# The hidden layer's last pair in the wide form, first pairs in another order, and gates moved to ScalarE

## The chip, the cores and the metric

The kernel runs on one core of one Trainium2 chip. A core has TensorE (PE in the profile; its weight loads are PEld), VectorE (DVE), ScalarE (ACT), GpSimd (POOL) and SyncE (SP). Each of them takes its instructions in the order in which the program wrote them. The metric is the device time of one execution in microseconds (us), lower being better. Before the change it is 849.36 us, the median of three runs (848.73 to 850.72).

## The reference

Two stages in float32. The first is attention with a mask from hashes: queries and keys of 4 batches, 8 heads, 768 positions and 64 features are hashed to 6 bits each, and a query sees the keys of its own bucket only. The second is a feed-forward layer on the 3072 x 512 result:

```python
def _moe_ref(x, w_in, w_out) -> np.ndarray:
    h = x @ w_in              # 3072 x 512 by 512 x 2048
    r = np.maximum(h, 0.0)
    g = r * r
    return (g @ w_out).astype(np.float32)
```

The change touches the second stage only, and the squares of a guard that looks for large inputs.

## The kernel before

Attention fills the first 314 us. Then the 3072 tokens are worked in three chunks of 1024 (`i` = 0, 1, 2, called chunk 0, 1, 2 here). Each chunk has a hidden part (x @ w_in and the gate, which is max(h, 0) * h) and a projection (`project`, g @ w_out).

**Products with seven multiplications.** Both use a form of Strassen's algorithm, in which a 2 x 2 block product takes 7 block products, some of sums of blocks. `product` writes one such step: seven groups of matmuls in the order 11, 21, t2, t1, t3, 22, t4, with sums of the moving operand called t1 to t4. Several of them go on accumulating in the same PSUM bank, so a bank's value is copied out by ScalarE between two groups (`keep`, the tiles `one`, `two`, `three`, `five`), and the later group must wait for that copy. With two levels, 49 products take the place of 64.

**The hidden part.** Chunk 0 uses one level (`hidden`). In chunks 1 and 2 the 16 row blocks of the hidden layer are made in four pairs of units (n = 0 to 3), each pair in two halves (`half` = 0, 1). A half has a weight unit `w_unit`. The results go to four tiles b11, b12, b21, b22, each with 8 slices; pair n makes slices r0 = n and r = 4 + n. `outer_steps` gives the first-level ("outer") groups, of two 128x512 matmuls each, in a bank `acc0`. `inner_steps` gives a second-level product of seven 128x256 matmuls, cut into four steps 0 to 3. A to E are five such inner products. `hidden_wide` (pairs 0 to 2) has 4 outer groups and 5 inner products; `hidden_pair` (pair 3) has 8 outer groups and the 3 inner products A, B, C.

An inner product's steps use two banks: one accumulates over steps 0 to 3 with a copy by ScalarE after each, the other is used in step 0 and again in steps 1 and 2. There are eight banks: `side_bank` 0 and 1 and two each of acc0, acc1, acc2. The step's copies land in tiles `h` (5 buffers), `three` (2), and `five` (1 buffer, for D).

**What follows a pair.** VectorE adds the inner result to the outer one and applies the gate in one instruction (`put`, `gated`). `gate_in` is the gate on ScalarE: a Relu and a Square in place. Differences b_t = b12 - b11 and b12 = b22 - b12, and `inner_sums` for the projection, follow on VectorE. What is left over from a pair is kept as a list of steps and written between the next pair's steps by `behind(m)`. D and E, the inner products with own factors, need the sums of a weight unit (`sum_unit`; made in chunk 1 on VectorE, stored by GpSimd to `w_in_49`, loaded in chunk 2), and sums of x (`sums_inner`).

**The projection.** Seven products (k = 0 to 6) take b11, b12, b_t, b22, b21, then b11 and b_t again, which by then hold a second and a fourth sum. Weights come as `leaf` tiles (7 buffers): five are loaded ahead, from the last half but one of the hidden part, by SyncE in chunk 0 and by ScalarE's queue in chunks 1 and 2; the others always by ScalarE's queue. `hook` is what VectorE does after the second group of a product.

**The guard.** `mark` squares a piece of q and k on ScalarE with an accumulated sum (32 in all, two buffers; each then has GpSimd load a later piece). Their maximum is read in chunk 2's product 4.

The order of everything is written out by hand: the order of calls in these functions is the order in each engine's queue.

Of the kernel before, what the change touches and what calls it, by code (L numbers as in the profile page):

```python
# [34 lines left out]
def kernel(  # L35
# [686 lines left out]
    def load_unit(n, pool=p_i):  # L722

        if n < NCHUNK * NR and n not in w_unit:
# [3 lines left out]
            if n < NR or pair == NQ - 1:  # L728
                m = 7 if n < NR else 4
                nc.sync.dma_start(out=w[:, 0:m], in_=w_in_7[r, :, 0:m])  # L730
                return
# [6 lines left out]
            if n >= 2 * NR:  # L738
                nc.sync.dma_start(out=five_six(w), in_=w_in_49[pair, :, 3 + half])
# [4 lines left out]
    def sum_unit(n):  # L744


        if NR <= n < 2 * NR and n % NR < NR - 2:
# [6 lines left out]
            nc.gpsimd.dma_start(out=w_in_49[pair, :, 3 + half], in_=five_six(w))  # L754
# [15 lines left out]
    with tc.manual_schedule():  # L770
# [201 lines left out]
        def product(n, w, at, bt, c11, c12, c21, c22, hook=None, last=False, beside=None, cuts=1):  # L972
# [16 lines left out]
            def keep(of, name):  # L989
                t = p_r.tile([P, 512], FP32, name=name, bufs=KEPT[name])[:, 0:w]  # L990
                nc.scalar.copy(out=t, in_=acc[of])  # L991
                return t
# [121 lines left out]
        w_inner, t_inner, spots, snaps, now, behind_pair = {}, {}, {}, {}, {}, {}  # L1114
# [77 lines left out]
        def sums_inner(i, js):  # L1192

            for j in js:
                y11, y12, y21, y22 = quarters_x(i, j)
                if j < 3:
                    tile = p_y.tile([P, NQ, QN], FP32, name=f"t{j}", **({"bufs": 2} if j < 2 else {}))
                    t = [tile[:, m] for m in range(NQ - 1)] + [y12]
                    spots[i, j] = tile[:, NQ - 1]
                else:  # L1200
# [3 lines left out]
                t_inner[i, j] = t  # L1204
# [5 lines left out]
        def inner_steps(i, j, side, w):  # L1210

            t1, t2, t4, t3 = t_inner[i, j]
            y11, _, y21, y22 = quarters_x(i, j)
            if i not in snaps:
                snaps[i] = [side_bank(m)[:, 0:QN] for m in range(2)]
            one = three = spots[i, side]
            hs = {}

            def new(unit):
                name = "five" if (j, unit) == (3, 0) else "three" if j == 4 else None
                if name:
                    return p_r.tile([P, 512], FP32, name=name, bufs=KEPT[name])
                return new_h()

            def mul(out, a, b, start, stop):
                nc.tensor.matmul(  # L1228
                    out=out, lhsT=w(a), rhs=b, start=start, stop=stop, skip_group_check=True
                )  # L1230

            def step_0():
                a0, a1 = (
                    ps_m.tile([P, 512], FP32, name=f"acc{m}")[:, 0:QN] for m in (0 if j == 4 else 1, 2)
                )
                mul(a0, 0, y11, True, False)
                nc.scalar.copy(out=one, in_=a0)
                mul(a1, 1, y21, True, True)
                hs[0] = new(0)
                nc.vector.tensor_tensor(out=hs[0][:, 0:QN], in0=a1, in1=one, op=ALU.add)  # L1240
                hs["a0"] = a0

            def step_1():
                last = hs["last"] = (
                    ps_m.tile([P, 512], FP32, name="acc2")[:, 0:QN] if j == 4 else snaps[i][side]
                )
                mul(hs["a0"], 4, t2, False, False)
                nc.scalar.copy(out=hs[0][:, QN:HN], in_=hs["a0"])
                mul(last, 3, t1, True, False)
                hs[1] = new(1)  # L1250
                nc.scalar.copy(out=hs[1][:, QN:HN], in_=last)

            def step_2():
                mul(hs["a0"], 5, t3, False, False)
                nc.scalar.copy(out=three, in_=hs["a0"])
                mul(hs["last"], 6, y22, False, True)

            def adds():
                for unit, by in (0, hs["last"]), (1, three):
                    add_in(hs[unit][:, QN:HN], by)  # L1260

            def step_3():
                mul(hs["a0"], 2, t4, False, True)
                nc.scalar.copy(out=hs[1][:, 0:QN], in_=hs["a0"])

            def put(unit, out, other):
                add_in(hs[unit], other)
                gated(out, hs[unit])

            return step_0, step_1, step_2, step_3, put, adds, hs  # L1270
# [43 lines left out]
        def hidden_wide(i, n, half):  # L1314

            r0, r = n, NQ + n
            w, acc, add, keep = outer_steps(i, n, half)
            own = own_factors(w, half)
            if half == 0:
                load_inner(i, n + 1)  # L1320
                load_third_inner(i, n + 1, nc.sync)
                now["A"] = inner_steps(i, 0, 0, w_inner[i, n][0])
                if n == 0:
                    sums_inner(i, (3,))
                now["D"] = inner_steps(i, 3, 1, lambda a: own[a])
            A, D = now["A"], now["D"]
            u0 = D[6]
            add(acc, 0, "11", True, False)
            one = keep(acc, "one")
            if half == 0:  # L1330
                A[0]()
                D[0]()
                if n == 0:
                    mark()
                    sums_inner(i, (4,))
                behind(0)
            else:
                B, C = inner_steps(i, 2, 0, w_inner[i, n][2]), inner_steps(i, 1, 1, w_inner[i, n][1])
                E = inner_steps(i, 4, 2, lambda a: own[a])
                B[0]()  # L1340
                C[0]()
                E[0]()
                A[4](1, b11[:, r], one)
                behind(2)
# [641 lines left out]
```

## Time and profile before

| what | value |
|---|---|
| median of the runs | 849.36 us |
| the profiled execution | 851.49 us |
| its span in the profile | 849.9 us |
| granted TensorE clock | 0.999 |
| TensorE busy | 841.6 us (99%) |
| VectorE busy | 758.5 us (89%) |
| ScalarE busy | 439.8 us (52%) |
| chunk 1, four pairs of the hidden part | 495.14 to 584.93 us |
| chunk 2, four pairs of the hidden part | 669.82 to 758.62 us |
| last chunk's projection starts | 758.62 us |

The profile is one execution, of 851.49 us; its span, 849.9 us, counts from the first to the last recorded instruction. Busy times of matmuls are modelled, so a short wait of TensorE hides in them and shows better as the distance between two pieces of the chain. In the rows, `L1228` is a line of the kernel, `out<-in` are tile names, and a bracket gives the idle time of the engine before that row and what ended it. A matmul in float32 counts as two instructions.

### The profile page before, as it was taken

Reading aid. Unit: us, or ns where it says so; the run is one execution under the profiler, and the core shown is the slowest. Engines: PE = TensorE matmul, PEld = TensorE weight load, DVE = VectorE, ACT = ScalarE, POOL = GpSimd, SP = SyncE. Lnnn points to the kernel's source line nnn. Section 1 sums busy time; section 2 is a strip of 40 time slices with the busy share of each in tenths; the row PEclk is TensorE's granted clock in tenths of the full one; section 3 lists DMA queues with packets and bytes.
Section 4 is the critical chain, followed back from the end, with each engine's and each line's share of the span. In section 5 each row is a group of like instructions: output and inputs, shape, how many; then the busy total and the mean of one; then the engine's idle time right before and its main releaser. Section 6 shows DMA issues by size and latency. Waiting matters only on the chain.

```text
span 849.9 us, 17478 instructions
## 1 busy us (share of the span) xinstructions
PE 841.6 (99%) x6698; PEld 555.4 (65%) x6698; DVE 758.5 (89%) x1087; ACT 439.8 (52%) x833; POOL 171.0 (20%) x289
## 2 busy tenths in 40 slices
PE   9999999999999999999999999999999999999997
PEld 4444444444475445544788877767888777768885
DVE  4898999999999988989899989988988988888876
ACT  5887777878777762222211146775232457753210
POOL 1321121303221201643121220001211300021103
PEclk9999999999999999999999999999999999999999
DMA  9966999989996426999977994418878964157666
GB/s 185 201 130 138 185 186 201 207 173 224 249 245 202 158 69 245 330 312 306 359 254 220 275 226 145 146 50 292 298 214 244 247 207 145 51 169 213 201 166 128
DMA packets 237304, 174.10 MB, mean 205 GB/s; under 512 B 165224, under 2 KB 195248, under 8 KB 237216
## 3 DMA queue, kind: packets, MB, share of 16 engines
q1 hardware_dynamic: 196976, 90.14, 43.3%
q0 software_dynamic: 16992, 44.02, 16.5%
q10 hardware_dynamic: 23248, 38.78, 14.7%
q8 instruction: 54, 0.88, 0.5%
q14 instruction: 34, 0.28, 0.1%
HBM read 129.51 MB, written 42.73 MB: 203 GB/s over the span
## 4 chain that ended last, share of the span: by engine, by line
PE 95%; DMA 2%; DVE 1%; ACTq 0%; issue 0%; ACT 0%; POOL 0%; SPq 0%; POOLq 0%; DVEq 0%
PE acc L984 40%; PE st L478 18%; PE xo L532 14%; PE acc L1228 10%; PE acc L1298 8%; PE last L1228 3%; PE tot L589 1%; PE hash L396 1%; DMA bits<-signed 1%; DMA out_dram<-h 1%; PE tp L342 0%; DMA qk_nat<-in_q_dram 0%; ACTq L1499 0%; DVE h L1522 0%; DVE o L1288 0%
## 5 line engine op out<-in xcount | busy, mean ns | idle before, releaser
L484 ACT ACTIVATE e<-st 128x768 f32<-128x768 f32 x192 | 155.5, 810 | 56.8 <-PE st L478 52.5
L532 PE MATMUL xo<-e,v_nat 64*64 64x385 f32 (+1 forms) x1520 | 156.7, 483 | 0.0
L984 PE MATMUL acc<-b,leaf 128*128 128x256 f32 x600 | 133.1, 379 | 0.0
L984 PEld LDWEIGHTS acc<-b,leaf 128*128 128x128 f32 x600 | 113.9, 190 | 16.1 <-issue 0.5
L478 PE MATMUL st<-feat 64*64 64x384 f32 x1056 | 109.3, 483 | 0.0
L444 POOL DMA_DIRECT2D bits<-signed x120 | 62.1, 522 | 196.5 <-ACT signed L433 194.7
L532 PEld LDWEIGHTS xo<-e,v_nat 64*64 64x64 f32 (+1 forms) x1520 | 58.5, 133 | 65.7 <-issue 54.7
L984 PE MATMUL acc<-t,leaf 128*128 128x256 f32 x336 | 76.1, 379 | 0.0
L984 PEld LDWEIGHTS acc<-t,leaf 128*128 128x128 f32 x336 | 63.7, 190 | 9.1 <-issue 0.3
L478 PE MATMUL st<-bits 64*64 64x384 bf16 x768 | 65.9, 324 | 0.4 <-DMA bits<-signed 0.4
L520 DVE TENSOR_TENSOR total<-total,e 128x1536 f32<-128x1536 f32 x32 | 56.0, 1750 | 7.6 <-ACT e L484 6.9
L1028 POOL DMA_DIRECT2D raw_qk<-in_q_dram x32 | 17.3, 541 | 212.3 <-ACT raw_qk L1033 209.8
L520 DVE TENSOR_TENSOR t_x<-t_x,e 128x1536 f32<-128x1536 f32 x32 | 55.8, 1744 | 3.9 <-ACT e L484 3.8
L478 PEld LDWEIGHTS st<-feat 64*64 64x64 f32 x1056 | 39.8, 133 | 25.6 <-issue 21.7
L984 PE MATMUL acc<-x,w_unit 128*128 128x512 f32 (+1 forms) x144 | 56.5, 546 | 0.0
L984 PE MATMUL acc<-b_t,leaf 128*128 128x256 f32 x240 | 53.8, 379 | 0.0
L991 ACT COPY two<-acc 128x256 f32<-128x256 f32 (+1 forms) x29 | 12.5, 431 | 75.2 <-PE acc L984 59.7
L1076 DVE SCALAR_TENSOR_TENSOR b<-h 128x512 f32<-128x512 f32 x72 | 49.1, 691 | 2.2
L991 ACT COPY one<-acc 128x256 f32<-128x256 f32 (+1 forms) x29 | 12.5, 431 | 72.6 <-PE acc L984 53.3
L984 PEld LDWEIGHTS acc<-b_t,leaf 128*128 128x128 f32 x240 | 45.6, 190 | 6.2
L478 PE MATMUL st<-t_x 64*64 64x384 f32 x480 | 48.9, 482 | 0.0
L478 PEld LDWEIGHTS <-bits 64*64 64x64 bf16 x768 | 24.6, 107 | 35.2 <-issue 32.8
(234 smaller groups left out, 1537.8 us busy)
## 6 DMA issues: line engine op xcount, KB each, us to landing
leaf<-w_out ACTq DMA_DIRECT2D x142, 256.0 KB, 3.4
raw<-in_moe_w_in_dram SPq DMA_DIRECT2D x8, 1024.0 KB, 6.4
raw<-in_moe_w_out_dram SPq DMA_DIRECT2D x8, 1024.0 KB, 7.5
w_unit<-w_in SPq DMA_DIRECT2D x8, 896.0 KB, 8.5
w_out<-sums POOLq DMA_DIRECT2D x16, 448.0 KB, 7.4
v_nat<-in_v_dram SPq DMA_DIRECT2D x16, 384.0 KB, 5.1
x_all<-x_raw SPq DMA_DIRECT2D x16, 384.0 KB, 3.2
raw_qk<-in_q_dram POOLq DMA_DIRECT2D x32, 192.0 KB, 3.6
```

Source lines behind the costliest of these rows:

```text
L396: nc.tensor.matmul(out=banks[g * NR_B:(g + 1) * NR_B, h, 0:HS], lhsT=projs[rows, h * D:h * D + NR_B], rhs=feat[pr][rows, w, c * HS:(c + 1) ...
L444: nc.gpsimd.dma_start(out=t[h * D:h * D + NBITS + 1, w, c * HS:(c + 1) * HS], in_=signed[pr % 2][at:at + NBITS + 1, h],)
L478: nc.tensor.matmul(out=st[k * HK:(k + 1) * HK, h, 0:HS], lhsT=src[1][rows, key], rhs=src[0][rows, cut], start=first, stop=not first, skip_ ...
L484: nc.scalar.activation(out=key_of(pr, kt)[:, :, i, 0:HS], in_=st[:, :, 0:HS], func=ACTF.Exp, scale=scale)
L520: nc.vector.tensor_tensor(out=totals[pr], in0=totals[pr], in1=e, op=ALU.add)
L532: return nc.tensor.matmul(out=outs[pr][h * D:(h + 1) * D, c, 0:HS + 1], lhsT=nat[pr, "v_nat"][rows, h, kt * D:(kt + 1) * D], rhs=key_of(pr ...
L984: nc.tensor.matmul(out=acc[to][:, at_c], lhsT=a(i), rhs=b(i)[:, at_c], start=first and i == 0, stop=last and i == n - 1, skip_group_check= ...
L991: nc.scalar.copy(out=t, in_=acc[of])
L1028: nc.gpsimd.dma_start(out=raw_qk[i][:, w], in_=flat[:, i * n:(i + 1) * n])
L1076: nc.vector.scalar_tensor_tensor(out=out, in0=h, scalar=0.0, in1=h, op0=ALU.max, op1=ALU.mult)
L1228: nc.tensor.matmul(out=out, lhsT=w(a), rhs=b, start=start, stop=stop, skip_group_check=True)
L1298: nc.tensor.matmul(out=to, lhsT=w[:, PLACE[a], f], rhs=bt[b](f), start=first and f == 0, stop=last and f == NFT // 2 - 1, skip_group_check ...
```

## The change

- `hidden_wide` makes all four pairs of chunk 2; `hidden_pair` is left to pair 3 of chunk 1. The last two weight units of chunk 2 get their sums from `sum_unit` on VectorE, in place. The work that follows the last pair (`edge`) is written into the first product of the projection, beside its copies (`then`).
- First pairs (n = 0): the order of half 0 becomes outer 11, A0, outer t2, A1, D0, A2, D1, A3, D2, D3, with the sums for D written after D0 and those for E before D3. Before, it was 11, A0, D0, t2, A1, D1, A2, D2, A3, D3 with the sums first.
- Other wide pairs: half 0 becomes A0, D0, 11, A1, D1, A2, D2, t2, A3, D3. In half 1, E uses the side banks.
- Gates: b11 is gated by ScalarE in wide pairs, b12's slice r in chunk 1 too. Leftovers are cut into six lists for `behind`.
- In later pairs of A and D, step 2 adds straight from the bank on VectorE and needs no copy by ScalarE.
- The second and fourth sums of the projection are made by quarters, at four places each. The five early leaf loads go to SyncE in all chunks. The guard's squares, three of them from the old pair 3, go to products 1 to 3 of chunk 2.

The core of the diff:

```diff
             def step_0():
-                a0, a1 = (
-                    ps_m.tile([P, 512], FP32, name=f"acc{m}")[:, 0:QN] for m in (0 if j == 4 else 1, 2)
-                )
-                mul(a0, 0, y11, True, False)
-                nc.scalar.copy(out=one, in_=a0)
-                mul(a1, 1, y21, True, True)
+                bank(0)
+                bank(1)
+                mul(0, 0, y11, True, False)
+                mul(1, 1, y21, True, True)
                 hs[0] = new(0)
-                nc.vector.tensor_tensor(out=hs[0][:, 0:QN], in0=a1, in1=one, op=ALU.add)
-                hs["a0"] = a0
+                nc.scalar.copy(out=hs[0][:, 0:QN], in_=banks[0])
+                add_in(hs[0][:, 0:QN], banks[1])
...
+                mul(0, 5, t_inner[i, j][3], False, False)
+                if direct:
+                    add_in(hs[1][:, QN:HN], banks[0])
+                else:
+                    nc.scalar.copy(out=hs[1][:, 0:QN], in_=banks[0])
...
+                A = now["A"] = inner_steps(i, 0, w_inner[i, n][0], n > 0)
+                D = now["D"] = inner_steps(i, 3, lambda a: own[a], n > 0)
                 if n == 0:
+                    add(acc, 0, "11", True, False)
+                    one = keep(acc, "one")
+                    A[0]()
+                    add(acc, 4, "t2", False, True)
+                    two = keep(acc, "two")
+                    A[1]()
+                    D[0]()
+                    mark()
                     sums_inner(i, (3,))
+                    A[2]()
+                    D[1]()
+                    A[3]()
+                    D[2]()
+                    sums_inner(i, (4,))
+                    D[3]()
+                else:
+                    A[0]()
+                    D[0]()
+                    add(acc, 0, "11", True, False)
+                    behind(0)
+                    one = keep(acc, "one")
+                    behind(1)
+                    A[1]()
+                    D[1]()
+                    A[2]()
+                    D[2]()
+                    behind(2)
+                    add(acc, 4, "t2", False, True)
+                    two = keep(acc, "two")
+                    A[3]()
+                    behind(3)
+                    D[3]()
+                now["two"] = two
+                add_to(b11[:, r0], A[4][0], one)
+                add_in(D[4][0], two)
+                gate_in(b11[:, r0])
+                if n == 0:
+                    mark()
+                behind(4)
+                sum_unit(i * NR + 2 * n + 1)
+                return
...
             add(acc, 0, "11", True, False)
             one = keep(acc, "one")
+            add_to(b11[:, r], A[4][1], one)
+            B[0]()
+            C[0]()
+            E[0]()
+            gate_in(b11[:, r])
+            behind(5)
+            sum_unit(i * NR + 2 * n + 2)
             add(acc, 4, "t2", False, True)
             two = keep(acc, "two")
...
+            steps = (
+                (sums_0, gates_0), (sums_1,),
+                (sums_2, gates_1, lambda: ahead(both), gates_2, gates_3),
+                (lambda: inner_sums(0, slice(n, n + 1)),), (gates_4,), (lambda: over(both),),
+            )
...
-                (hidden_wide if s // 2 < NQ - 1 else hidden_pair)(i, s // 2, s % 2)
+                (hidden_wide if i > 1 or s // 2 < NQ - 1 else hidden_pair)(i, s // 2, s % 2)
...
-                        load_leaf(n, i == 0)
+                        load_leaf(n, True)
```

In it `sums_0` adds the second slices of b12 (in chunk 2 with VectorE's gate, `put`) and b22, `sums_1` and `sums_2` make the two slices of b21, `gates_0` to `gates_4` are ScalarE's gates of b22, b12 (chunk 1 only), b22, b21 and b21, `ahead` makes b_t and `over` the new b12, each for both slices in one instruction.

More of the change, by code (lines that the diff above doesn't have):

```diff
@@ L1208, in sums_inner, with inner_steps, bank @@
                 minus(t[3], y22, y12)
-        def inner_steps(i, j, side, w):
-            t1, t2, t4, t3 = t_inner[i, j]
+        def inner_steps(i, j, w, direct=False):
             y11, _, y21, y22 = quarters_x(i, j)
[L1216 to L1219, printed above, removed]
+            hs, banks = {}, {}
+            def bank(m, later=False):
+                side = m if j == 4 else j // 3 if later and j in (0, 3) else None
+                t = side_bank(side) if side is not None else ps_m.tile([P, 512], FP32, name=f"acc{m + 1}")
+                banks[m] = t[:, 0:QN]
             def new(unit):
                 name = "five" if (j, unit) == (3, 0) else "three" if j == 4 else None
+                if (j, unit) == (3, 1):
+                    return p_y.tile([P, HN], FP32, name="other")
                 if name:
@@ L1255, in step_2 @@
[L1255 to L1260, printed above, removed]
-            def step_3():
[L1263 to L1268, printed above, removed]
@@ L1328, in hidden_wide @@
+            u0 = D[4]
             add(acc, 0, "11", True, False)
             one = keep(acc, "one")
[L1330 to L1344, printed above, removed]
-                sum_unit(i * NR + 2 * n + 2)
+            add_to(b11[:, r], A[4][1], one)
```

231 lines of the change are left out of this document (144 added, 87 removed).

## The prediction

> **What bounds the kernel now.** I read the page's busy shares and its chain first, then the chain in order of time, then windows by stage, last the timeline of single engines. The page:
>
> ```profile
> span 849.9 us, 17478 instructions
> PE 841.6 (99%) x6698; PEld 555.4 (65%) x6698; DVE 758.5 (89%) x1087; ACT 439.8 (52%) x833; POOL 171.0 (20%) x289
> ...
> PE 95%; DMA 2%; DVE 1%; ACTq 0%; issue 0%; ACT 0%; POOL 0%; SPq 0%; POOLq 0%; DVEq 0%
> ```
>
> TensorE is the path. The change is worth the matmuls it removes, less every wait that it puts in front of a matmul. ScalarE is half idle on average, so what counts is not how much it has to do but where an instruction stands in its queue. The windows (a pair of wide half steps, then pair 3; PE, weight loads, VectorE, ScalarE, GpSimd):
>
> ```profile
> core 0: us, PE busy (x) PEld busy (x) DVE busy (x) ACT busy (x) POOL busy (x), PEclk, DMA share, GB/s
> 517.12:539.31 22.19, 22.19 (x87) 16.26 (x87) 20.81 (x47) 14.74 (x35) 1.08 (x2) 1.00 0.43 139
> 561.50:584.93 23.43, 23.25 (x76) 13.89 (x75) 19.78 (x37) 17.16 (x39) 3.20 (x7) 1.00 0.44 146
> 669.82:691.79 21.97, 21.97 (x87) 16.34 (x87) 16.79 (x38) 12.55 (x32) 2.13 (x4) 1.00 0.75 212
> 713.77:735.75 21.98, 21.98 (x87) 16.35 (x87) 19.22 (x39) 15.89 (x37) 0.00 (x0) 1.00 0.40 129
> 735.75:758.62 22.87, 22.87 (x75) 13.97 (x75) 20.25 (x38) 17.28 (x39) 2.13 (x4) 1.00 0.36 116
> ```
>
> Chain pieces (start, us, what):
>
> ```profile
> 528.31 2.81 PE acc L1228 x12
> 577.54 0.04 ACT one L1309
> 578.02 0.39 ACT t L1255
> 578.45 1.13 PE acc L1228 x4
> 681.01 2.59 PE acc L1228 x12
> 735.75 1.72 PE acc L1298 x4
> 737.46 0.86 PE acc L1228 x4
> ```
>
> An outer product (two 128x512 matmuls) takes 1.72 us, an inner one 0.86/2 = 0.43. A wide pair is 4 outer products and 35 inner ones, 6.88 + 15.05 = 21.9: the windows of the last chunk hold no stall at all. Chunk 1 has some: 2.81 against 2.59, that is 0.22 in each of pairs 1 and 2, and 23.43 - 22.87 = 0.56 in pair 3. So at most 1.0 us of waiting is there to be won.
>
> **The change, part by part.** t is counted from the start of a pair on TensorE.
>
> *Last pair of chunk 2 in the wide form:* 22.87 becomes 21.98, -0.89. What must follow it now lies inside the first product of the projection, which TensorE runs in seven groups of 1.73 us. VectorE, by the prices below: from the put of b12 at -0.15 eleven instructions of 512 columns, three of 256, one sum out of a bank and one of 1024 to the last two differences of b12, which are there 10.9 us into the product; their first reader, the fourth matmul of the second product, comes at 12.1 + 1.3 = 13.4. ScalarE: from b12's sum (4.3) on, three gates, the copies of `two` and `five` and a mark put the end of the copy of `three` at 9.9, and the group that overwrites its bank starts at 10.36. Cost 0 with 0.5 us to spare; without that cover up to 1.
>
> *Leaf loads from ScalarE's queue to SyncE's, chunk 1's pair 3:* the copy of `one` at 577.54 stood behind five leaf loads that waited for buffers; the chain runs through it into TensorE's late start. On SyncE they block only what is queued behind them there, the next chunk's unit and the stores of the results, due a product later. The new order of `behind` puts three gates (3.7 us) ahead of the second half's `one` in that pair, which ends at 16.1 by the prices below where its bank is wanted at 18.1: cost 0. So -0.56, bounds 0 to -0.56.
>
> *Gates of b11 on ScalarE, wide pairs 1 to 3.* In the new half 1 TensorE runs outer 11, six inner products of B, C, E, then t2 into the bank of 11. So t2, due at 9.48 + 1.72 + 2.59 = 13.79, must wait until ScalarE has copied `one`. That copy now stands behind the gates of b11 and b21, and the b11 gate waits for a VectorE sum near the end of a long queue. The queue's prices (VectorE, pair 3 of chunk 2 starts at 735.75, pair 2 at 713.77):
>
> ```profile
> 713.62 0.68 DVE L1273 TENSOR_TENSOR h<-h 128x512 f32<-128x512 f32 x1
> 714.34 0.69 DVE L1076 SCALAR_TENSOR_TENSOR b<-h 128x512 f32<-128x512 f32 x1
> 714.95 0.68 DVE L1288 TENSOR_TENSOR b<-five,three 128x512 f32<-128x512 f32 x1
> 715.55 0.68 DVE L1288 TENSOR_TENSOR b<-h,three 128x512 f32<-128x512 f32 x1
> ...
> 717.48 0.42 DVE L1240 TENSOR_TENSOR h<-acc,t 128x256 f32<-128x256 f32 x1
> 717.81 0.42 DVE L1240 TENSOR_TENSOR five<-acc,t 128x256 f32<-128x256 f32 x1
> ...
> 720.67 0.42 DVE L676 TENSOR_TENSOR t<-b 128x256 f32<-128x256 f32 x1
> 721.13 0.42 DVE L676 TENSOR_TENSOR t<-b,t 128x256 f32<-128x256 f32 x1
> 721.47 0.42 DVE L676 TENSOR_TENSOR b<-b 128x256 f32<-128x256 f32 x1
> ...
> 724.34 0.68 DVE L1273 TENSOR_TENSOR h<-h,one 128x512 f32<-128x512 f32 x1
> ...
> 765.73 1.22 DVE L676 TENSOR_TENSOR b<-b,t 128x1024 f32<-128x1024 f32 x1
> 766.86 1.22 DVE L676 TENSOR_TENSOR t<-b 128x1024 f32<-128x1024 f32 x1
> ```
>
> From start to start: 512 columns 0.60, or 0.72 if the next needs the result; 256 columns 0.33, or 0.46; 1024 columns 1.13. ScalarE and the weight loads:
>
> ```profile
> 673.14 0.85 ACT L1033 ACTIVATE raw_qk<-raw_qk 128x768 f32<-128x768 f32 x1
> 673.88 0.19 ACT L1033 ACTIVATION_READ_ACCUMULATOR raw_qk<-raw_qk 128x1 f32 x1
> ...
> 751.72 0.65 ACT L1278 ACTIVATE b<-b 128x512 f32<-128x512 f32 x1
> 752.41 0.63 ACT L1081 ACTIVATE b<-b 128x512 f32<-128x512 f32 x1
> 752.94 0.57 ACT L1309 COPY five<-acc 128x512 f32<-128x512 f32 x1
> 753.41 0.37 ACT L1264 COPY h<-acc 128x256 f32<-128x256 f32 x1
> 753.67 0.38 ACT L1248 COPY h<-acc 128x256 f32<-128x256 f32 x1
> ...
> 756.21 0.30 PEld L1298 LDWEIGHTS acc<-t_x,w_unit 128*128 128x128 f32 x2 [0.21 <-ACT two L1309]
> ```
>
> A gate (Relu, Square) holds ScalarE 752.94 - 751.72 = 1.22, a 256 copy 0.26, a mark 0.93. A hand-over from one engine to the next is 578.45 - 578.41 = 0.04 (578.41 is where the row at 578.02 ends), here taken as 0.05. After a wait TensorE loses more than the wait: the weight load stood still too (756.21), and the piece at 578.45 took 1.13 for 0.86, so +0.27.
>
> VectorE's queue around the pair's start is unchanged up to the sum `b<-five,three`, at 714.95 - 713.77 = 1.18, done 1.86. `five` has one buffer, so D's copy into it runs 1.9 to 2.3 and its add starts at 2.33. Then, in chunk 2: b12's put 0.72 + 0.60, b22 0.60, tmp 0.72, b21 0.60, two 0.60, four adds of 256 1.32, b21 0.60, b_t 1.13, three inner sums 1.12. The first add's 0.33 and these 8.0 put the b11 sum at 10.7 to 11.4. Two gates (2.44) and the copy (0.58) end at 14.4; TensorE goes on at 14.8: 1.0 late, three times, +3.0. Chunk 1 does b12's gate on ScalarE: 0.7 less on VectorE, so 0.35 late; twice that, less the old 0.22 each (the E banks that caused it are now the side banks), +0.26. Bounds: 0.4 to 1.4 a pair in chunk 2, 0 to 0.8 in chunk 1, from one VectorE instruction more or less.
>
> *First pair of chunks 1 and 2:* none stalled before (21.97). Three waits are new. (a) D1 follows A2 (0.86 us) but needs the second of D's inner sums, now issued behind D0's add: 0.04 + 0.33 + 0.46 + 0.42 against 0.86, with the restart +0.65. (b) D3 follows D2 by one matmul of 0.43, while its bank is copied in 0.04 + 0.38 + 0.05: restart included, +0.3, bounds 0 to 0.3. (c) half 1's `one`: E's four sums (0.46 + 0.46 + 0.33 + 0.33) now stand ahead of the b11 sum, which waits in order for D2's copy (9.7, after the two delays above), takes two adds of 256, those four and its own 0.68, and ends at 12.7; the gate, the second mark (0.93) and the copy of `one` end at 15.5, TensorE goes on at 15.8, and t2 was due at 13.79 + 0.95 = 14.7: +1.1, bounds 0.6 to 1.5. Together 2.05 a chunk, twice, +4.1.
>
> *Free moves:* the second and fourth sums of the projection split in quarters cost the same 4.5 us of VectorE where no product waits; the guard's squares go to chunk 2's first products, each 0.93 in ScalarE slack of some 1.3 us a group, and their loads on GpSimd's queue meet nothing else there. The last units' factor sums, eight VectorE adds of 128x128, stand behind the b11 sum. Two loads replace one per unit on SyncE, most of a pair ahead. Taken at 0; all of it late would be 1.
>
> Sum: -0.89 - 0.56 + 3.0 + 0.26 + 4.1 = +5.9. The profiled execution took 851.49 (span 849.9), 2.1 over the median 849.36; against itself it becomes 857.4, against the median 855.3.
>
> [...]
>
> **The rivals.**
> 1. *Nothing waits, faster.* VectorE reaches the b11 sum about 1.1 us sooner, so `one` is copied before t2 is due, in first pairs too. It decides when that sum ends before 10.4. For it: ScalarE idles 1.7 us before the gate. Against: the queue has only 0.25 us of idle time to lose, and before, that sum began at 724.34 - 713.77 = 10.6, as in my count. Then -0.89 - 0.56 - 0.44 = -1.9: 847.5.
> 2. *Only (a) and (b) remain:* -1.9 + 1.9 = 0: 849.4, the same.
> 3. *TensorE restarts at once after a wait*, its weights loaded: eleven restarts of 0.27 less, -3.0: 852.3. Against it the two rows above.
> 4. *Delays add up:* ScalarE, late at `two` as well, holds B and C copies, a mark waits for its load. One more 0.4 in each of ten half steps: 859.3. VectorE's idle time (21.98 - 19.22 = 2.8 us a pair, nearly all in half 1) speaks against it.
>
> **How the numbers follow.** Forecast 0.55 (its own range 852.9 to 858), rival 1 0.15, 2 0.10, 3 0.12, 4 0.08. Slower 0.55 + 0.12 + 0.08 = 0.75, same 0.10, faster 0.15, with 0.2% (1.7 us) as what a measurement tells apart. Leaving out rival 1 and the top of rival 4, the range is 848.5 to 859.5.
>
> **What would show it.** Right: stretches of 23.0 for wide pairs 1 to 3 of chunk 2, of 22.3 for those of chunk 1 and of 24.0 for the two first pairs, with the chain passing through the copy of `one`, the gate of b11 and VectorE's sums there; no leaf load on ScalarE ahead of `one` in chunk 1's last pair; a projection without a gap after the last pair. Wrong: wide pairs still at 21.98, which would mean that VectorE gets to b11 by 10.4.

## The result and the profile after

The changed kernel takes 857.36 us (median of four runs, 856.22 to 858.82), the kernel before 849.17 us beside it: a ratio of 1.0094, 95% interval 1.0073 to 1.0115, so 6 to 10 us slower. The profiled execution took 856.92 us. From its page, the span, the busy times and the shares of the chain:

```profile
span 855.4 us, 17531 instructions
...
PE 843.1 (99%) x6710; PEld 556.5 (65%) x6710; DVE 748.2 (87%) x1081; ACT 461.5 (54%) x873; POOL 171.0 (20%) x289
...
PE 82%; DVE 10%; ACT 3%; DMA 2%; issue 1%; SPq 0%; POOL 0%; ACTq 0%; DVEq 0%; POOLq 0%
```

TensorE held 95% of the chain before and holds 82% now; VectorE went from 1% to 10%, although it is less busy. The windows of the changed kernel, one row for each pair or projection, show where (columns as in the prediction):

```profile
core 0: us, PE busy (x) PEld busy (x) DVE busy (x) ACT busy (x) POOL busy (x), PEclk, DMA share, GB/s
495.12:519.18 24.06, 22.82 (x88) 16.02 (x87) 18.03 (x48) 14.68 (x36) 3.27 (x7) 1.00 0.63 177
519.18:541.50 22.32, 22.25 (x88) 16.27 (x87) 18.73 (x42) 18.20 (x41) 1.08 (x2) 1.00 0.43 138
541.50:563.82 22.32, 22.25 (x87) 16.27 (x87) 17.82 (x38) 18.21 (x41) 0.54 (x1) 1.00 0.43 127
563.82:586.70 22.88, 22.88 (x75) 13.98 (x75) 17.93 (x31) 17.06 (x39) 3.22 (x7) 1.00 0.44 150
586.70:672.52 85.82, 85.11 (x393) 74.35 (x393) 79.23 (x120) 24.12 (x60) 20.48 (x37) 1.00 0.86 259
672.52:696.58 24.06, 22.83 (x87) 16.02 (x87) 14.81 (x36) 14.58 (x36) 2.54 (x5) 1.00 0.69 198
696.58:719.47 22.89, 22.24 (x87) 16.26 (x87) 17.50 (x35) 17.27 (x39) 0.00 (x0) 1.00 0.42 135
719.47:742.36 22.89, 22.24 (x88) 16.26 (x87) 18.39 (x39) 17.27 (x39) 0.00 (x0) 1.00 0.39 124
742.36:765.26 22.90, 22.25 (x88) 16.27 (x87) 18.40 (x39) 17.27 (x39) 0.00 (x0) 1.00 0.26 87
765.26:850.20 84.94, 84.92 (x393) 74.08 (x392) 73.36 (x113) 26.71 (x63) 16.49 (x29) 1.00 0.71 199
```

Against before: first pairs 24.06 for 21.98 and 21.97, pairs 1 and 2 of chunk 1 22.32 for 22.19, its last pair 22.88 for 23.43, its projection 85.82 for 84.89, pairs 1 and 2 of chunk 2 22.89 for 21.98, its last pair 22.90 for 22.87, its projection 84.94 for 84.68. The sum, 355.08 for 348.16, is 6.92 more. In a wide pair of chunk 2 the chain runs as the prediction had it (start, us, what): the b11 sum, two gates, the copy of `one`, and t2, whose piece of the chain takes 1.98 us where that of an undisturbed group takes 1.72:

```profile
707.38 0.61 DVE b L1300
708.02 0.64 ACT b L1290
708.68 0.63 ACT b L1084
709.31 0.53 ACT b L1290
709.86 0.63 ACT b L1084
710.49 0.48 ACT one L1321
...
711.01 1.98 PE acc L1310 x4
```

The pair began at 696.58, so the sum ran from 10.8 to 11.4 and t2 began at 14.43 instead of 13.79. The 0.26 that t2 takes more is called its restart here. It has two parts. In TensorE's timeline the undisturbed t2 at 703.31 has a row of 1.88 us, and the next row starts 1.72 us after it, before the first has ended; the late t2 at 711.01 has 1.98 and 1.82. So 0.10 is a longer group, and 0.16 is the overlap with the group before, which the row after this wait doesn't have. The list of waits for TensorE counts five such waits (us in total, times, longest):

```profile
PE acc L1310 <- ACT one L1321: 3.1, 5, 0.7
```

In chunk 1's first pair TensorE's timeline shows the three waits (a), (b) and (c):

```profile
502.70 0.67 PE L1242 MATMUL acc<-o,w_unit 128*128 128x256 f32 x2 [0.61 <-DVE o L676]
...
505.12 0.70 PE L1242 MATMUL acc<-o,w_unit 128*128 128x256 f32 x2
...
510.72 1.98 PE L1310 MATMUL acc<-t_x,w_unit 128*128 128x512 f32 x4 [0.60 <-ACT one L1321]
```

Two places were not foreseen. The first product of chunk 1's projection has two waits (TensorE), and the reason stands some 12 us earlier on VectorE and ScalarE:

```profile
591.81 2.43 PE L985 MATMUL acc<-t,leaf 128*128 128x256 f32 x10 [0.36 <-DVE t L676]
598.03 5.42 PE L985 MATMUL acc<-b,leaf 128*128 128x256 f32 x24 [0.35 <-issue]
```
```profile
577.06 1.23 DVE L676 TENSOR_TENSOR b_t<-b,b 128x1024 f32<-128x1024 f32 x1 [1.58 <-ACT b L1084]
...
580.17 0.42 DVE L1285 TENSOR_TENSOR h<-h 128x256 f32<-128x256 f32 x1 [0.56 <-ACT h L1268]
```
```profile
578.76 0.63 ACT L1084 ACTIVATE b<-b 128x512 f32<-128x512 f32 x1
579.30 0.57 ACT L1321 COPY one<-acc 128x512 f32<-128x512 f32 x1
579.77 0.38 ACT L1268 COPY h<-acc 128x256 f32<-128x256 f32 x1
```

The three gates left from pair 2 end at 579.3; behind them stand `one` and then the copies of B2 and C0, for which VectorE waits (580.17). It never catches up before the projection. The other place is the last projection, where a square of the guard, moved there by the change, waits for its load and holds the copy of `five`; TensorE's 24 matmuls there take 5.64 us, where e3 below has 5.34 (ScalarE, then TensorE):

```profile
784.76 0.84 ACT L1036 ACTIVATE raw_qk<-raw_qk 128x768 f32<-128x768 f32 x1 [1.82 <-DMA raw_qk<-in_k_dram]
...
785.60 0.35 ACT L992 COPY five<-acc 128x256 f32<-128x256 f32 x1
```
```profile
784.09 5.64 PE L985 MATMUL acc<-b,leaf 128*128 128x256 f32 x24
```

### The profile page after: what moved, and what is told of

Its sections match the earlier page's. It is cut to its first block, busy times and chain, and to the rows that moved or that the text cites. A ratio compares the mean times of both kernels' runs of the same rounds, so it can differ in the third digit from the quotient of the medians.

```text
span 855.4 us, 17531 instructions
## 1 busy us (share of the span) xinstructions
PE 843.1 (99%) x6710; PEld 556.5 (65%) x6710; DVE 748.2 (87%) x1081; ACT 461.5 (54%) x873; POOL 171.0 (20%) x289
## 4 chain that ended last, share of the span: by engine, by line
PE 82%; DVE 10%; ACT 3%; DMA 2%; issue 1%; SPq 0%; POOL 0%; ACTq 0%; DVEq 0%; POOLq 0%
PE acc L985 37%; PE st L478 18%; PE xo L532 14%; PE acc L1242 5%; PE acc L1310 3%; DVE b L1300 2%; PE last L1242 2%; PE tot L589 1%; DVE h L1285 1%; DVE b_t L676 1%; PE hash L396 1%; ACT b L1290 1%; ACT b L1084 1%; DVE t L676 1%; DMA bits<-signed 1%
## 5 line engine op out<-in xcount | busy, mean ns | idle before, releaser
L985 PEld LDWEIGHTS acc<-x,w_unit 128*128 128x128 f32 x144 | 27.3, 190 | 26.6 <-issue 25.2
```

The lines of the kernel that those rows point to most:

```text
L985: nc.tensor.matmul(out=acc[to][:, at_c], lhsT=a(i), rhs=b(i)[:, at_c], start=first and i == 0, stop=last and i == n - 1, skip_group_check= ...
```

## The experiments

Each experiment is the changed kernel with one edit, or several named ones. The table gives the stretches between the first rows of each stage in TensorE's timeline: hidden part and projection of chunk 1, hidden part of chunk 2, its projection up to the first transpose of the tail, and their sum, all in us. Each ratio in the text goes by runs of the kernel before that were taken beside the experiment (medians of 849.41 to 850.96 us), not by the 849.17 above; where a time comes from one run, the traces carry the argument.

| run | hidden 1 | projection 1 | hidden 2 | projection 2 | sum |
|---|---|---|---|---|---|
| before | 89.79 | 84.89 | 88.80 | 85.39 | 348.87 |
| changed | 91.57 | 85.83 | 92.74 | 85.68 | 355.82 |
| e1_gates_behind_one | 90.89 | 85.84 | 90.01 | 85.40 | 352.14 |
| e2_first_pair_order | 89.92 | 86.13 | 90.67 | 85.39 | 352.11 |
| e6_b12_on_scalar | 91.57 | 86.25 | 91.00 | 85.40 | 354.22 |
| e9_mark_alone | 90.89 | 85.84 | 92.07 | 85.40 | 354.20 |
| e7_last_pair_narrow | 91.58 | 86.03 | 92.73 | 85.45 | 355.79 |
| e8_leaf_loads_on_scalar | 93.55 | 86.22 | 96.22 | 85.39 | 361.38 |
| e3_gates_and_order | 89.29 | 85.83 | 87.99 | 85.40 | 348.51 |
| e5_pair3_gates_later | 90.06 | 84.61 | 87.98 | 85.39 | 348.04 |
| e10_all_places | 88.86 | 86.69 | 87.97 | 85.40 | 348.92 |
| e11_sums_early | 91.58 | 87.34 | 92.75 | 85.39 | 357.06 |
| e12_sums_early_in_chunk_0 | 89.64 | 84.61 | 87.99 | 85.87 | 348.11 |
| e13_squares_one_copy_later | 89.65 | 84.61 | 87.99 | 85.39 | 347.64 |

Where nothing differs, the hidden parts agree within 0.02; chunk 1's projection, while it has waits, scatters by 0.4 (85.83 to 86.25). The last projection takes 85.39 to 85.45 in every row but two, 85.68 in the changed kernel and 85.87 in e12. Eleven of these kernels have the guard's square at the same place in it. In nine of them TensorE lost nothing, in e5 for one after the square had waited 1.17 us for its load; in the changed kernel it waited 1.82 and in e12 2.01. So that 0.3 us belongs to single executions, and the effect of an edit on a hidden part is better read from its own column than from the sum.

**Gates behind `one`.** In half 0 the gates (and a first pair's second mark) go, and half 1 gets them:

```diff
-                gate_in(b11[:, r0])
-                if n == 0:
-                    mark()
-                behind(4)
                 sum_unit(i * NR + 2 * n + 1)
...
             one = keep(acc, "one")
+            behind(4)
             add_to(b11[:, r], A[4][1], one)
             B[0]()
             C[0]()
             E[0]()
+            gate_in(b11[:, r0])
+            if n == 0:
+                mark()
             gate_in(b11[:, r])
```

> The gates of b11 (first half) and b21 and, in first pairs, the second mark stand on ScalarE behind the second half's copy of `one` instead of ahead of it; nothing else differs from the changed kernel. Theory (ScalarE's order makes t2 late): the pairs of chunk 2 after the first go from 22.89 to about 22.0 us, pairs 1 and 2 of chunk 1 from 22.32 to 22.0, the first pairs lose their part (c), about 1.1 each of 24.06, and keep (a) and (b); 357.4 - 0.9 x 3 - 0.3 x 2 - 1.1 x 2 in the third digits, that is some 5.5 us less than the changed kernel, about 852. Rival (VectorE's queue is what is too long, ScalarE only waits for it): t2 is free earlier but a later group of the pair waits for VectorE instead, the pairs stay within 0.3 us of 22.89 and the time stays at about 857. Second rival (the wide last pair and its work in the projection cost the time): the pairs gain at most 1 us in all.

Measured 854.66 us, 1.0053 of before (1.0039 to 1.0067). The wide pairs do what the theory says, the first pair does not:

```profile
495.98:519.98 24.00, 22.83 (x88) 16.01 (x87) 18.02 (x48) 14.41 (x36) 3.28 (x7) 1.00 0.66 183
696.71:718.72 22.01, 22.01 (x87) 16.26 (x87) 17.59 (x35) 16.79 (x39) 0.00 (x0) 1.00 0.43 140
```

VectorE's queue, which the rival blamed, is as long as it was (17.59 us busy for 17.50); ScalarE's order alone was worth 0.9 us a pair. The sum falls by 3.68, not by 5.5, and 0.28 of that is the last projection, which the edit doesn't touch. In the first pair t2 is on time, but gate, mark and gate now stand between E's copies and those of B, and TensorE waits one step later (ScalarE's rows, then TensorE's):

```profile
510.86 0.63 ACT L1290 ACTIVATE b<-b 128x512 f32<-128x512 f32 x1
...
512.06 0.83 ACT L1036 ACTIVATE raw_qk<-raw_qk 128x768 f32<-128x768 f32 x1
...
512.89 0.61 ACT L1290 ACTIVATE b<-b 128x512 f32<-128x512 f32 x1
...
514.54 0.38 ACT L1258 COPY h<-acc 128x256 f32<-128x256 f32 x1
```
```profile
514.97 1.13 PE L1242 MATMUL acc<-x,leaf 128*128 128x256 f32 x4 [0.54 <-ACT h L1258]
```

**The first pairs' order.** Only the branch for n = 0 differs:

```diff
                 if n == 0:
+                    sums_inner(i, (3,))
                     add(acc, 0, "11", True, False)
                     one = keep(acc, "one")
                     A[0]()
+                    D[0]()
+                    mark()
+                    sums_inner(i, (4,))
                     add(acc, 4, "t2", False, True)
                     two = keep(acc, "two")
                     A[1]()
-                    D[0]()
-                    mark()
-                    sums_inner(i, (3,))
-                    A[2]()
                     D[1]()
-                    A[3]()
+                    A[2]()
                     D[2]()
-                    sums_inner(i, (4,))
+                    A[3]()
                     D[3]()
```

> Only the first pairs of chunks 1 and 2 differ from the changed kernel: their first half runs outer 11, A0, D0, outer t2, A1, D1, A2, D2, A3, D3 again, with D's sums of x ahead of all and E's behind D0. Theory: (a) and (b) go wholly, and (c) too, since the b11 sum comes some 2 us sooner on VectorE: first pairs 24.06 -> 22.0 us, two times 2.05, so about 4 us less than the changed kernel, 853.3; the other pairs stay at 22.89 and 22.32. Rival (only (a) and (b) are due to the order, the gate and the mark ahead of `one` still hold t2): first pairs about 23.0, some 2 us less, 855.3. Rival (first pairs are slow for the gate on ScalarE alone): no more than 0.5 us.

Measured 853.93 us, 1.0044 of before (1.0028 to 1.0060). Chunk 2's first pair, 671.43 to 693.41 on the chain, is 21.98, so the order held all of (a), (b) and (c). Chunk 1's stays at 22.4: VectorE is still busy with chunk 0's results there (below), and TensorE waits 0.18 us for one of its sums at 501.59.

**b12's gate on ScalarE in chunk 2 too.**

```diff
-                if i == 1:
-                    add_to(b12[:, r], hB[1], u0[1])
-                else:
-                    put(hB[1], b12[:, r], u0[1])
+                add_to(b12[:, r], hB[1], u0[1])
...
-                if i == 1:
-                    gate_in(b12[:, r])
+                gate_in(b12[:, r])
```

> Only the gate of b12's second slice in chunk 2 differs: it runs on ScalarE as in chunk 1, which takes one instruction of 128x512 (0.60 to 0.72 us) out of VectorE's queue ahead of the b11 sum. Theory (the b11 sum at the end of VectorE's queue sets when `one` is copied): pairs 1 to 3 of chunk 2 go from 22.89 to about 22.3 us, as in chunk 1. Rival (ScalarE's amount of work ahead of `one` sets it): one more gate of 1.2 us there leaves them at 22.89 or makes them up to 1.2 longer.

Measured 855.86 us in one run; the pairs fall from 22.89 to 22.32 (22.31), chunk 1's figure:

```profile
697.93:720.24 22.31, 22.24 (x87) 16.25 (x87) 16.92 (x34) 18.21 (x41) 0.00 (x0) 1.00 0.43 138
720.24:742.56 22.32, 22.25 (x88) 16.27 (x87) 17.83 (x38) 18.21 (x41) 0.00 (x0) 1.00 0.41 127
```

One VectorE instruction less ahead of the b11 sum moved t2 by 0.57, while ScalarE had 1.2 us more to do. So two things make the wait together: a late VectorE sum, and a place in ScalarE's queue that makes `one` wait for it.

**The mark alone** (e9): `mark()` of a first pair behind `E[0]()` in half 1, the gate where it was.

```diff
                 gate_in(b11[:, r0])
-                if n == 0:
-                    mark()
                 behind(4)
...
             E[0]()
+            if n == 0:
+                mark()
             gate_in(b11[:, r])
```

> The changed kernel, with the second mark of the first pairs alone moved behind the copies of B, C and E in the second half; the gate of b11 stays ahead of `one`. Theory (the mark's 0.93 is most of the first pairs' part (c) of 1.1): t2 is 0.2 late instead of 1.1, with its restart, so the first pairs go from 24.06 to about 23.3, and the later copies of B wait for nothing. Rival (what follows E's copies on ScalarE is full already): the 0.9 is found again as a wait in front of B's steps and the pairs stay at 24.0.

Measured 855.29 us in one run; the sums of hidden 1 and 2 fall by 0.68 and 0.67, the first pairs take 23.38 and 23.37. The mark was most of (c). This and e2 don't contradict each other: t2 is late by what VectorE's late sum and the mark behind it make together, and either an earlier sum or no mark in front of `one` takes all or most of it.

**Both together.** As the first two, with `if n == 0:` keeping the gate and the mark in half 0 and `if n > 0:` moving it.

> The first two experiments together, with the gate of b11 and the mark of a first pair left in their place in front of `one` (there the first experiment only moved the wait of 0.95 us to the copies of B, while with the old order of steps the b11 sum comes early enough). Theory: every wide pair at 22.0 us in both chunks, so 0.9 x 3 + 0.3 x 2 + 2.08 x 2 = 7.4 us less of the changed kernel's 355.08 us between the start of chunk 1's hidden part and the last matmul of the projection, which is 347.7 against 348.16 before; time 849, the same as before (ratio 0.998 to 1.002). Rival (the delays overlap, or VectorE's queue is late at the next place): at least 1 us of it stays, 850 or more.

Measured 850.10 us, 0.9996 of before (0.9987 to 1.0006): what the change lost is back. By the table's measure the theory gives 355.82 - 7.4 = 348.4, and 348.51 came: all wide pairs are at 22.0 but chunk 1's first, where 0.42 is left at D1 (a wait of 0.18 and its restart), and the last projection is 0.28 shorter, since the square's late load did not hold TensorE in this trace.

**Pair 2's gates later in chunk 1's last pair.**

```diff
+            if (i, n) == (1, NQ - 2):
+                steps = steps[:2] + (steps[2][:3], steps[3], (gates_2, gates_3, gates_4), steps[5])
...
                 behind(3)
+                behind(4)
                 put(A[4][1], b11[:, r], one)
                 put(B[4][0], b12[:, r0], now["two"])
-                behind(4)
                 behind(5)
```

> As the run before, and in chunk 1's narrow last pair the three gates left from pair 2 (b22 twice, b21) stand on ScalarE behind the copies of B2 and C0 of the second half instead of ahead of the copy of `one`. Theory (the two waits of the first projection product come from VectorE's sums, which waited for B2's and C0's copies behind these gates): the waits of 0.36 and 0.35 us with their restarts go, the stretch from chunk 1's pair 3 to chunk 2 falls from 108.7 or 109.0 to 107.8 us; 1 us less than the run before, 848 or 0.998 to 0.999 of before. Rival (VectorE is late there for the idle 1.58 us in front of the differences b_t, which wait for b12's gate): the waits stay, no difference to the run before.

Measured 850.61 us, 0.9998 (0.9990 to 1.0007). Both waits of the first product are gone, projection 1 takes 84.61, though VectorE still idles 1.58 us ahead of b_t: the gates ahead of `one` were the cause. Part of it came back as a new wait in the pair, since the three gates now hold `two`, so the sum falls by 0.47 against e3 and not by 1, and the ratio does not show it:

```profile
584.40 1.98 PE L1310 MATMUL acc<-t_x,w_unit 128*128 128x512 f32 x4 [0.45 <-ACT two L1321]
```

**The second and fourth sums put back** (e11: this alone, in chunks 0 and 1; e10: with it and one gate of b21 behind C3, on top of e5).

```diff
                 if k == 0:
-                    second_sum(*Q12)
+                    if more:
+                        for some in UPPER, LOWER:
+                            second_sum(some, slice(0, HN))
+                    else:
+                        second_sum(*Q12)
                     inner_sums(2)
```

The other places get `and not more`, the fourth sum the same behind product 2.

> The changed kernel, with only the second and fourth sums of chunks 0 and 1 put behind products 0 and 2 again. Theory (these moves cost only what VectorE's lag costs at the end of chunk 0's projection): VectorE's last transposes of chunk 0 end 2.4 us sooner against the start of chunk 1, the wait of 0.17 near 493 with its restart goes, the pairs stay at 24.06, 22.32, 22.32 and the projection of chunk 1 keeps its two waits; 0.35 us less. Rival (the moves are free): the wait near 493 stays.

> As e5_pair3_gates_later, with two more places changed: the gate of b21's second slice left from pair 2 goes behind the copies of C3 at the end of chunk 1's last pair (it made `two` late there, a wait of 0.45 us and a restart of 0.27), and in chunks 0 and 1 the second and fourth sums of the projection stand behind the products 0 and 2 again, in two halves each, as before the change. Theory (the sums put later make VectorE 2.4 us later at the end of chunk 0's projection, which costs a wait of 0.18 with a restart there and one of 0.18 with a restart at D1 of chunk 1's first pair): chunk 1's first pair goes from 22.39 to 22.0 us, its last pair with the projection from 108.27 to about 107.6, the wait of 0.18 near 494 goes; from the start of chunk 1's hidden part to the first transpose of the tail 346.9 us against 348.87 before, time 0.9975 to 0.9985 of before. Rival (VectorE is late again elsewhere in the projections of chunks 0 and 1 with the sums put early): no less than e5_pair3_gates_later, 0.999 to 1.001.

e11 took 858.90 us in one run, e10 851.09 us, 1.0002 (0.9991 to 1.0013). The wait near 493, 0.17 us in the changed kernel, went in both, and e10's chunk 1 lost its wait at D1 (hidden 1 88.86), so that much of the theory holds. But projection 1 grew to 87.34 and 86.69, so e10's sum is 348.92 and not 346.9: the rival. e11's sum rises by 1.24 where 0.35 less was expected; neither its theory nor its rival had that. In e11 the second sum holds VectorE for 4.49 us in the second product, the differences of that product's operand come late, and TensorE waits (VectorE, then TensorE):

```profile
603.35 4.49 DVE L676 TENSOR_TENSOR b<-b,b_t 128x2048 f32<-128x2048 f32 x2
...
611.29 1.22 DVE L676 TENSOR_TENSOR b<-b,t 128x1024 f32<-128x1024 f32 x1
```
```profile
612.61 1.97 PE L985 MATMUL acc<-b,leaf 128*128 128x256 f32 x8 [1.27 <-issue]
```

In e10, where the hidden part ends sooner, TensorE also waits for leaf loads (0.38 us at 594.10, 0.15 at 596.22). The quarters were not a free move: behind a hidden part that ends with VectorE late they save over 1 us, and in chunk 0 they cost a little (e12 below has 0.42 less in hidden 1 than e5).

**Leaf loads on ScalarE again:** `load_leaf(n, i == 0)`.

> The changed kernel, with the five early leaf loads of chunks 1 and 2 in ScalarE's queue again. Theory (the copy of `one` in chunk 1's pair 3 was late for them): they stand behind the three gates now, take some 0.5 us of the queue each, and the copy of `one` at 15.5 us into the pair moves to about 17 or 18; the pair grows by 0 to 0.5 us and the waits of VectorE in the first product by 1 to 2. Chunk 2's last pair, whose gates of b11 already hold its `one`, has them behind its half 0 too and grows by up to 2. Rival (the gates cover the loads): all stretches within 0.1 us of the changed kernel's 22.88, 85.82 and 22.90.

Measured 863.28 us in one run, 5.9 over the changed kernel's median. The direction is the theory's, the size is not: chunk 1's last pair grows by 1.98 and chunk 2's by 3.48 (1.79 of longer waiting and 1.69 behind it, for which see the last section). ScalarE's rows show five issues of 0.48 us, in order, ahead of `one`:

```profile
579.01 2.39 ACTq L1572 DMA_DIRECT2D leaf<-w_out  x5
581.45 0.58 ACT L1321 COPY one<-acc 128x512 f32<-128x512 f32 x1 [1.89 <-DMA leaf<-w_out]
```

and TensorE stands still for C0's copy in chunk 1 and for `one` in chunk 2:

```profile
582.36 0.70 PE L1242 MATMUL acc<-t,leaf 128*128 128x256 f32 x2 [1.60 <-ACT h L1268]
```
```profile
761.13 2.99 PE L1310 MATMUL acc<-t_x,w_unit 128*128 128x512 f32 x4 [2.44 <-ACT one L1321]
```

**The last pair narrow again:** `hidden_pair` for chunk 2's pair 3, with its loads, sums and marks. It reads t1 and t3 of x after sums for D and E have overwritten a quarter of each; the instructions are those of whole values.

```diff
-                    (hidden_wide if i > 1 or s // 2 < NQ - 1 else hidden_pair)(i, s // 2, s % 2)
+                    (hidden_wide if s // 2 < NQ - 1 else hidden_pair)(i, s // 2, s % 2)
```

> Chunk 2's last pair is made by hidden_pair again, with its three marks, its weight units loaded with stored sums and the gates left to the pair itself; the rest is the changed kernel. Theory (the wide last pair saves 0.89 of matmuls and loses as much to its late t2): the pair stays at 22.9 us, and the projection of chunk 2 loses its 0.26 or takes up to 0.9 as chunk 1's does behind its narrow pair; the time stays within 1 us of 857. Rival (the wide last pair and what it leaves to the projection is where the time went): 4 us or more come back.

Measured 856.53 us in one run; the pair takes 22.88, hidden 2 92.73 for 92.74. In this kernel the wide last pair neither gains nor loses: 0.89 of matmuls saved, 0.90 lost to the late t2. With the gates moved (e3) it gains: hidden 2 is 87.99 for 88.80 before.

**A version that beats both.** e12 is e5 with the sums put back in chunk 0 alone (`i == 0` for `more` in the diff above); e13 also moves the three squares of chunk 2's products one copy later:

```diff
-                then = {"two": mark} if i == NCHUNK - 1 and 0 < k < 4 else {}
+                then = {"five": mark} if i == NCHUNK - 1 and 0 < k < 4 else {}
```

> As e5_pair3_gates_later, with the second and fourth sums put early again in chunk 0's projection alone, where VectorE is not late from a narrow pair. Theory: the wait near 494 and the one at D1 of chunk 1's first pair go as in e10_all_places (22.39 -> 22.0 us), and chunk 1's projection keeps the late sums and has no wait, 84.6 us; 347.6 us from the start of chunk 1's hidden part to the first transpose of the tail against 348.87 before, 0.35 more ahead of it, time 0.998 to 0.999 of before. Rival (what remains of the gain is lost ahead of the hidden part or below what the runs scatter): 0.999 to 1.001.

> As e12_sums_early_in_chunk_0, with the three squares in products 1 to 3 of chunk 2 behind the copy of `five` instead of the copy of `two`, 1.73 us later. Theory (in product 1 this square waits 1.17 to 2.01 us for its load, and the copy of `five` behind it makes TensorE wait, 0.29 us in the changed kernel and 0.47 in e12_sums_early_in_chunk_0): the last projection takes 85.4 us again instead of 85.87, its square waits 0.5 us at most; 0.9980 to 0.9990 of before, no more than 0.5 us from e12_sums_early_in_chunk_0. Rival (the load, not the place, is late: it now holds the copy of `three`): the projection stays over 85.6.

e12: 849.34 us, 0.9984 (0.9975 to 0.9992). e13: 848.74 us, 0.9987 (0.9977 to 0.9997). Each is a little faster than before, by 0.16% and 0.13%, with intervals from 0.03 to 0.25%; these overlap, so which of the two is the better isn't settled. In e12's profiled execution the first square in product 1 waited 2.01 us for its load and the last projection took 0.48 more than its best. In e13 the square still waits, more than the 0.5 expected, but nobody waits for it, and the projection takes 85.39. Nine of the eleven kernels with the square at its old place do as well, so this one trace shows that a wait of 1.56 us costs nothing at the new place, but not that the move gains anything:

```profile
779.53 0.84 ACT L1036 ACTIVATE raw_qk<-raw_qk 128x768 f32<-128x768 f32 x1 [1.56 <-DMA raw_qk<-in_k_dram]
```

## Why the prediction was right, and where it was not

- *Gates of b11 in chunk 2:* 23.0 foretold, 22.89 to 22.90 measured, with the b11 sum at 10.8 to 11.4 (foretold 10.7 to 11.4). e1 undoes it, e6 takes 0.57 of the 0.91. The sum's end at 11.4 rules out rival 1, which needed it before 10.4, and the late t2 rules out rival 2, in which only (a) and (b) remain.
- *Chunk 1's wide pairs:* 22.3 foretold, 22.32 measured; e1 brings 22.01.
- *First pairs:* 24.0 foretold, 24.06 measured. The parts fit less well than their sum: (a) 0.61 of waiting and 0.24 of restart, 0.85 where 0.65 was put down; (b) 0.30 for 0.3; (c) 0.60 and 0.26, 0.86 for 1.1; and 0.07 at the first half's t2, which was not listed. The errors of (a) and (c) offset each other: TensorE went on with t2 at 15.9 us into the pair, 15.8 being foretold, so what (a) took more is missing from (c). e2 takes all of it in chunk 2, and e9 shows the mark as 0.7 of (c).
- *Last pair of chunk 2:* -0.89 and +1.0 foretold, +0.03 measured; the work in the first product behind it made no wait, as foretold.
- *Leaf loads:* -0.56 foretold, 23.43 to 22.88 measured. In the trace before, the five loads hold ScalarE's queue for 3.33 us from 574.17, one of them for 1.51; that they waited for buffers it does not show. What the step did not say is that in the new kernel the old place would cost ten times that in two chunks (e8, sum 361.38 for 355.82).
- *The third and fourth rival:* that TensorE restarts at once falls on every late t2 (rows of 1.96 to 1.99 us in the changed kernel, 1.88 where it was in time): a chunk 2 pair lost 0.91 with a wait of 0.65. The 0.27 of the forecast was the right size, but 0.16 of it is the lost overlap shown above. The load of t2's weights waited too, 1.05 us by its row below, so these weights were not loaded when the wait ended. The fourth rival, delays that add up in every half step, falls on the pairs, which came out within 0.11 us of their forecast.

```profile
711.01 0.30 PEld L1310 LDWEIGHTS acc<-t_x,w_unit 128*128 128x128 f32 x2 [1.05 <-ACT one L1321]
```

The hidden parts grew by 5.72, where 5.91 was put down. Two terms that were costed at nothing were not nothing. "The new order of `behind` puts three gates (3.7 us) ahead of the second half's `one` in that pair, which ends at 16.1 by the prices below where its bank is wanted at 18.1: cost 0": the copy did end at 16.05 and the bank was in time, but the copies of B2 and C0 stand behind `one`, and VectorE waits for those. It made the projection 0.93 longer; e5 shows the cause. This step failed, because it followed the bank and not the queue. And the guard's squares, whose "loads on GpSimd's queue meet nothing else there": with two buffers and three squares a product, the load came late for its square, by 1.82 us here, 2.01 in e12 and 1.17 in e5, but of the eleven traces that have it at this place it cost TensorE time in two only, 0.29 us in this one. Together 1.22, against a sum of +5.9 and a trace that grew by 6.95 (355.82 - 348.87).

The forecast gave 857.4 us against the profiled execution and 855.3 against the median. The profiled execution of the changed kernel took 856.92, the median is 857.36. That 857.4 meets the median to the digit is luck, since it was not worked out for it; the median grew by 8.2 us where 5.9 was forecast.

The medians differ by 1.2 us more than the traces between the start of chunk 1 and the tail. That remainder is not located; the interval of the ratio, 6.2 to 9.8 us, takes it in. The other stretches differ between executions by as much: the code ahead of chunk 1 is the same in the changed kernel and in e1, e2, e3 and e5 to e9, and chunk 1 starts at 494.05 to 496.59 us in these nine traces; the tail takes 6.05 us in the trace before and 4.62 in the changed kernel's.

## What to carry to other kernels

A copy that frees an accumulator belongs ahead of any work that waits for another engine: with `one` ahead of the gates (e1) the wide pairs of chunk 2 went from 22.9 to 22.0 us. When something is put ahead of a copy in an engine's queue, look not only at the bank that the copy frees but at every copy queued behind it and at the engine that waits for those (VectorE, 0.56 us before 580.17); and look one copy further when it is moved back, since e1's first pairs (0.54 us) and e5 (0.45) each found the next one. A cost that comes in some executions only, as that of the square's late load (in two of eleven traces), has to be looked for in several before it is called a cost of the change. Work that is moved "for free" can be what covers a delay elsewhere, and shows its worth only in the new kernel (the quarters: with the sums put back, e11's projection 1 takes 87.34 us for 85.83).

## What was not expected of the hardware

A long wait was followed, in one run, by a lower clock. In e8 chunk 2's t2 took 2.99 us after a wait of 2.44, where the waits of 0.65 us left 1.98; from t2's start to the projection it took 9.99 us, where the changed kernel takes 8.30. The windows give the granted clock (PEclk):

```profile
core 0: us, PE busy (x) PEld busy (x) DVE busy (x) ACT busy (x) POOL busy (x), PEclk, DMA share, GB/s
758.00:761.00 3.00, 0.69 (x4) 0.26 (x2) 0.00 (x0) 1.29 (x4) 0.00 (x0) 1.00 0.58 167
761.00:764.00 3.00, 2.87 (x5) 1.25 (x6) 2.82 (x5) 2.10 (x6) 0.00 (x0) 0.66 0.78 271
764.00:767.00 3.00, 3.00 (x12) 2.55 (x11) 0.69 (x1) 2.07 (x5) 0.00 (x0) 0.77 0.01 4
767.00:771.00 4.00, 4.00 (x20) 3.51 (x19) 2.08 (x6) 2.34 (x7) 0.00 (x0) 1.00 0.00 0
```

The clock was 0.66 and then 0.77 behind the wait, and full again in the row that starts 6 us later; the wait of 1.60 us at 582.36 left it at 1.00. A gap of 2.44 us in TensorE's matmuls came before a lower clock here, once. In the changed kernel, after the wait of 0.65 us in the same place, the clock stays at 1.00 (757 to 765 us); no run had a length between these two there.
